# RWKV-5 and mixture of depths on one core: a bonus summed by the tensor engine, and rank counts with one compare a block

## The chip, the cores and the metric

The kernel runs on one core of one Trainium2 chip. The metric is the device time of one execution in microseconds (us). The core's engines are PE (TensorE, matrix products; PEld is its weight load), DVE (VectorE), ACT (ScalarE), POOL (GpSimd) and SP (SyncE, which issues most DMAs). Each runs its own queue of instructions in order and waits on semaphores for the others.

## The reference

Batch 4, 8 heads, 768 steps, 48 channels a head. First a linear attention with decay `w` and a bonus `u` for the current step, then a router which picks the 128 best tokens of each batch and passes only these through a small MLP (F = 1024).

```python
for t in range(S):
    cur = einsum('bhd,bhe->bhde', u[None] * kt, vt)
    y[:, :, t] = einsum('bhd,bhde->bhe', rt, state + cur)
    state = w[None, :, :, None] * state + einsum('bhd,bhe->bhde', kt, vt)
# x = y as (B, S, 384)
scores = einsum('bsd,d->bs', x, w_gate)
out = x.copy()
for b in range(B):
    top_idx = argpartition(-scores[b], capacity)[:capacity]
    ye = maximum(x[b, top_idx] @ w1, 0.0) @ w2
    g = 1.0 / (1.0 + exp(-scores[b, top_idx]))
    out[b, top_idx] = x[b, top_idx] + g[:, None] * ye
```

The bonus of a step is one number a head, the sum over the 48 channels of r·u·k, which multiplies v of the same step.

## The kernel before, in words

The work is cut into 24 units of 128 steps (`NU`; `NC` = 6 units a batch, `T` = 128), each with all 8 heads as `NP` = 4 pairs. The tokens of a unit are cut once more into two chunks of 64. The order of all instructions is written out by hand (`manual_schedule`), so every engine's queue is the order in which the functions are called. One turn of the main loop, iteration n, works on three units at once:

- `states(n-1)` (L322): what earlier chunks give to unit n-1, into the PSUM tiles y0 and y1, of which there is one each. A tiny ACT copy, the mark (L326), follows.
- `products(n)` (L282): k·v sums of both chunks, into the PSUM tile rp. `scores(n)` (L292): r·k inside a chunk, into other columns of rp.
- `added(n, c)` (L303, DVE): the running state plus a chunk's sum. For c = 1 four ACT activations scale it into z of the next unit (L310); the last unit of a batch has no c = 1.
- `masked(n)` (L297, DVE): copies the scores below the diagonal from rp over `at`, whose diagonal holds the bonus.
- `values(n-1)` (L338): at times v, added into y0 and y1. `finish(n-1)`: three ACT copies (L355, L357) take y0 and y1 to x, and SP stores x.
- `turn(n+1)`: transposes keys (L260) and r (L265) to put channels on partitions; ACT copies the keys to kh (L270), and `turned` (L275, DVE) scales r to rh.
- For the bonus: `bonus(n+2)` (L237, L243) multiplies r, k and u on POOL with the tokens on partitions, `bonus_sum(n+1)` (L247) reduces over channels on DVE to du, and `diagonal(n+1)` (L251, POOL) spreads du on the diagonal of `at`. `scaled(n+2)` (L233, POOL) scales the keys to kw.

The routing of a batch goes with the units of the next. `score(n-1)` (L367, DVE) is the router's score. For each block j of 128 tokens `scores_along` (L378, PE) turns the scores into a row, and `compare` (L385, L387, DVE) compares this row with each of the j+1 blocks so far, one instruction each, and counts. `count` and `rank` (L392, L396, L399, L402) give each token its rank; `match` (L423) makes a one-hot of the rank, `pick` (L429) its token and score, `fetch` (L445, POOL's indirect DMA) the token's row xr. `hidden` (L472) and `expert` (L481) are the MLP on PE, in pieces from iteration 11 on; `leave` (L489, L491) stores the result. The call `work_at(n, where)` inserts these pieces.

SP's loads of unit n+4 (`load`, parts 0 to 3: k, r and two halves of v) are each held until a named DVE instruction is done, and so are the 16 pieces of w1 and w2 (`weights`), two in each of iterations 6 to 13. r and k have five buffers, v has six.

Of the kernel before, what the change touches and what calls it, by code (L numbers as in the profile page):

```python
# [7 lines left out]
F32 = mybir.dt.float32  # L8
# [9 lines left out]
def kernel(  # L18
# [52 lines left out]
    nc.vector.memset(mark, 0.0)  # L71
    ub = const.tile([128, H, D], F32)
    wg = const.tile([128, Dm], F32)
    for i, q in enumerate((nc.sync, nc.scalar)):
        q.dma_start(
            out=wp[i * PAD : i * PAD + D, 0, :],
            in_=bass.AP(tensor=w.tensor, offset=w.offset + i * D, ap=[[1, D], [2 * D, NP]]),
        )
    nc.scalar.activation(mark, mark, AF.Sigmoid)
# [48 lines left out]
    load(0, 1)  # L128
    nc.sync.dma_start(out=ub, in_=bass.AP(tensor=u.tensor, offset=u.offset, ap=[[0, 128], [D, H], [1, D]]))
    load(0, 2)  # L130
# [58 lines left out]
    for i in range(NW - 1):  # L189
        nc.vector.tensor_mul(wp[:, i + 1, :], wp[:, i, :], wp[:, i, :])  # L190
        h = 1 << i
        if h < MID:
# [4 lines left out]
                         back[:, None, :, None].to_broadcast([128, 2, NP, MID]))  # L197
    wc = wp[:, NW - 1, :]
    gone = const.tile([128, 1], F32)
    nc.gpsimd.tensor_copy(gone, tr[:, 0, 0:1])  # L200
# [7 lines left out]

    counts = [const.tile([128, NC, NC + 2], F32, name=f"counts{i}") for i in range(2)]
    slots = const.tile([128, 128], F32)  # L210
# [3 lines left out]
    def late_tables():  # L214
        nc.gpsimd.iota(slots, pattern=[[1, 128]], base=0, channel_multiplier=0,
                       allow_small_or_imprecise_dtypes=True)
        for x in counts:
            nc.gpsimd.memset(x, 0.0)
            nc.gpsimd.iota(x[:, :, NC + 1], pattern=[[128, NC]], base=0, channel_multiplier=0,
                           allow_small_or_imprecise_dtypes=True)  # L220
        nc.gpsimd.iota(tok[:, :, 0], pattern=[[0, NU]], base=0, channel_multiplier=1,
                       allow_small_or_imprecise_dtypes=True)
        nc.gpsimd.iota(tok[:, :, 1], pattern=[[T, NU]], base=0, channel_multiplier=0,
                       allow_small_or_imprecise_dtypes=True)
# [4 lines left out]

    KH, RH, RK, RKU, DU, AT, ZA, ZB, YP = ({} for _ in range(9))  # L230

    def scaled(n):
        nc.gpsimd.tensor_mul(kws[n % 3][:, :, :D], KIN[n], wk)  # L233

    def bonus(n):
        rk = RK[n] = work.tile([128, H, D], F32, name="rk")
        nc.gpsimd.tensor_mul(rk, rpads[n % NIN][:, :, :D], KIN[n])  # L237
        if n:
            bonus_scaled(n, nc.gpsimd)

    def bonus_scaled(n, engine):
        RKU[n] = work.tile([128, H, D], F32, name="rku")
        engine.tensor_mul(RKU[n], RK[n], ub)  # L243

    def bonus_sum(n):
        DU[n] = work.tile([128, 2, NP], F32, name="du")
        return nc.vector.tensor_reduce(DU[n], RKU[n].rearrange("t (p i) d -> t i p d", i=2), axis=AX.X, op=OP.add)  # L247

    def diagonal(n):
        AT[n] = work.tile([128, H, C], F32, name="at", bufs=3)  # L250
        nc.gpsimd.tensor_mul(AT[n], dia[:, None, :].to_broadcast([128, H, C]),  # L251
                             DU[n].rearrange("t i p -> t (i p)")[:, :, None].to_broadcast([128, H, C]))

# [121 lines left out]
    def scores_along(b, j):  # L375
        p = psum.tile([128, 512], F32, name="m", bufs=4)
        SR[b, j] = p[:, :128]
        nc.tensor.transpose(SR[b, j], sc[b][:, j : j + 1].to_broadcast([128, 128]), ident)  # L378

    def compare(b, j):  # L380

        if j == 0:
            GT[b] = work.tile([128, NC, NC, 128], BF16, name="gt")
        for c in range(j + 1):
            nc.vector.tensor_scalar(GT[b][:, c, j, :], SR[b, j], sc[b][:, c : c + 1], None, op0=OP.is_gt, op1=OP.add,  # L385
                                    accum_out=counts[b % 2][:, c, j : j + 1])
        nc.vector.scalar_tensor_tensor(scr[:, :128], SR[b, j], sc[b][:, j : j + 1], earlier, op0=OP.is_equal,  # L387
                                       op1=OP.mult, accum_out=counts[b % 2][:, j, NC : NC + 1])

# [3 lines left out]

    def rank(b):
        p = psum.tile([128, 512], F32, name="m", bufs=4)
        nc.tensor.matmul(out=p[:, 0:1], lhsT=GT[b][:, 0, 0, :], rhs=ones[:, 1:2], start=True, stop=True)  # L396
        for c in range(1, NC):
            for cc in range(c):
                nc.tensor.matmul(out=p[:, c : c + 1], lhsT=GT[b][:, cc, c, :], rhs=ones[:, 0:1],  # L399
                                 start=(cc == 0), stop=(cc == c - 1))  # L400
        q = work.tile([128, NC], F32, name="qq")
        nc.vector.tensor_add(q, p[:, :NC], QQ[b])  # L402
        QQ[b] = q
# [11 lines left out]

    def match(b, z):
        oh = OH[b, z] = work.tile([128, NC, 128], BF16, name="oh")
        q = QQ[b]
        if z:
            q = work.tile([128, NC], F32, name="qz")  # L420
            nc.vector.tensor_scalar(q, QQ[b], float(-128 * z), None, op0=OP.add)
        for c in range(NC):
            nc.vector.tensor_scalar(oh[:, c, :], slots, q[:, c : c + 1], None, op0=OP.is_equal, op1=OP.add,  # L423
                                    accum_out=found[:, c : c + 1])
# [117 lines left out]

    bonus(0)
    warm(10)
# [5 lines left out]
    turned(0, pr)  # L550
    bonus_scaled(0, nc.vector)
    bonus_sum(0)
    earlier = const.tile([128, 128], F32)
    nc.vector.tensor_scalar(earlier, jp, 0.0, None, op0=OP.is_lt)
    ones = const.tile([128, 2], BF16)
    nc.vector.memset(ones[:, 0:1], -1.0)
    nc.vector.memset(ones[:, 1:2], 0.0)
    scaled(0)
    diagonal(0)
    scaled(1)  # L560
    bonus(1)
    for n in range(NU):
        if n == 2:
            late_tables()
        b, c = divmod(n, NC)
        if c == 0:
            ZA[n] = zt
        if n:
            behind = states(n - 1)
        products(n)  # L570
        scores(n)
        work_at(n, "scores")
        load(n + 4, 0, added(n, 0))
        op = masked(n)
        load(n + 4, 2, op)
        weights(2 * (n - NC), op)
        if n:
            values(n - 1, behind)
            finish(n - 1)
        if n + 1 < NU:  # L580
            pr = turn(n + 1)
        if c < NC - 1:
            added(n, 1)
        if n + 1 < NU:
            load(n + 4, 1, turned(n + 1, pr))
            load(n + 4, 3, bonus_sum(n + 1))
        if n + 2 < NU:
            scaled(n + 2)
        if n + 1 < NU:
            diagonal(n + 1)  # L590
        if n + 2 < NU:
            bonus(n + 2)
        work_at(n, "turn")
        if n:
            weights(2 * (n - NC) + 1, score(n - 1))
        if n + 1 < NU:
            work_at(n, "end")
# [71 lines left out]
```

## Time and profile before

| | us |
|---|---|
| median of 3 runs | 172.78 |
| lowest, highest | 168.68, 177.97 |
| the profiled execution | 166.79 |
| its span, first to last instruction | 165.0 |
| PE busy | 148.1 |
| DVE busy | 123.6 |
| POOL busy | 116.5 |
| ACT busy | 72.3 |

The mean granted clock of PE was 0.969 in this execution. A line of the page's groups gives the line of code, the engine and operation, the tile written and those read, the shape, the count, then busy time in us and the mean in ns of one, then the engine's idle time ahead of these and what ended it. A line of a timeline gives the start in us, the duration, the engine, the line and the operation; a line of the chain of waits gives the start, the time on the chain, and what ran.

### The profile page before, as it was taken

The numbers are of one execution on the slowest core, as the hardware profiler recorded it, in microseconds if no ns is written. First come the engines' busy times: TensorE is split into PE (matmuls) and PEld (weight loads), VectorE is DVE, ScalarE is ACT, GpSimd is POOL, SyncE is SP. The second block draws the span as 40 slices with busy tenths as digits, with TensorE's granted clock in tenths as the row PEclk, the third lists the DMA queues.
The fourth block names the chain that finished last, engine by engine and source line by source line (L and its number), as shares of the span: only waits on it lengthen the run. The fifth ranks groups of instructions, "written<-read, shape, count | busy, mean of one in ns | idle before, by whom it ended". The sixth has DMA issues, their size and how long they took to land.

```text
span 165.0 us, 7987 instructions
## 1 busy us (share of the span) xinstructions
PE 148.1 (90%) x3278; PEld 122.0 (74%) x3278; DVE 123.6 (75%) x478; ACT 72.3 (44%) x227; POOL 116.5 (71%) x158
## 2 busy tenths in 40 slices
PE   6869998887798599999999989999999978999970
PEld 2468887775686598999868859999787758968830
DVE  7854887989999948979999599799986987801010
ACT  6813765536455334454545244347524632202100
POOL 8499999998988897959878699968897621122002
PEclk9987999999999759999999999999999999999999
DMA  4988987978898899879988789978701321011001
GB/s 78 205 173 166 180 176 171 198 138 177 185 224 209 183 241 246 173 181 225 215 181 195 185 199 264 197 155 174 193 4 54 92 89 67 0 48 50 2 0 48
DMA packets 84325, 24.51 MB, mean 149 GB/s; under 512 B 76481, under 2 KB 83905, under 8 KB 84289
## 3 DMA queue, kind: packets, MB, share of 16 engines
q1 hardware_dynamic: 83568, 22.42, 61.0%
q0 software_dynamic: 512, 1.57, 3.1%
q8 instruction: 26, 0.43, 1.1%
q14 instruction: 11, 0.08, 0.1%
q10 hardware_dynamic: 208, 0.00, 0.1%
HBM read 18.48 MB, written 5.51 MB: 145 GB/s over the span
## 4 chain that ended last, share of the span: by engine, by line
PE 45%; POOL 16%; DVE 13%; issue 12%; DMA 5%; ACT 5%; POOLq 1%; ACTq 0%; DVEq 0%
PE m L472 9%; PE rp L282 7%; PE y L322 5%; PE m L260 5%; PE rp L292 5%; PE y L338 5%; PE m L265 4%; POOL rk L237 4%; PE m L481 4%; POOL at L251 4%; DVE gt L385 4%; POOL rku L243 3%; DMA rpad<-in_r_dram 3%; POOL kw L233 3%; ACT vpad L156 2%
## 5 line engine op out<-in xcount | busy, mean ns | idle before, releaser
L251 POOL TENSOR_TENSOR at<-dia,du 128x512 f32<-128x512 f32 x24 | 25.6, 1066 | 12.5 <-DVE du L247 10.3
L243 POOL TENSOR_TENSOR rku<-rk,ub 128x384 f32<-128x384 f32 x23 | 25.4, 1104 | 1.8
L385 DVE TENSOR_SCALAR_CACHE_REDUCE gt<-m,sc 128x128 bf16<-128x128 f32 x84 | 24.5, 344 | 1.3 <-PE m L378 1.3
L237 POOL TENSOR_TENSOR rk<-rpad,kin 128x384 f32<-128x384 f32 x23 | 24.3, 1056 | 1.3 <-DMA rpad<-in_r_dram 1.3
L367 DVE SCALAR_TENSOR_TENSOR scr<-x,wg 128x384 f32<-128x384 f32 x24 | 21.9, 912 | 2.6 <-DVE scr L387 0.5
L282 PE MATMUL rp<-vpad,kw 128*48 128x96 f32 x384 | 22.0, 260 | 1.9 <-POOL kw L233 1.2
L310 ACT ACTIVATE z<-g,wp 128x48 f32<-128x48 f32 x80 | 20.2, 326 | 7.3 <-DVE g L303 7.3
L472 PE MATMUL m<-xt,w 128*128 128x128 f32 x192 | 23.3, 276 | 0.0
L233 POOL TENSOR_TENSOR kw<-kin,wk 128x384 f32<-128x384 f32 x23 | 23.0, 1001 | 0.1
L472 PEld LDWEIGHTS m<-xt,w 128*128 128x128 f32 x192 | 22.3, 192 | 0.5 <-ACT xt L463 0.5
L481 PE MATMUL m<-w,ht 128*128 128x384 f32 x64 | 22.6, 491 | 0.1
L355 ACT COPY x<-y 128x192 f32<-128x192 f32 x24 | 7.7, 319 | 29.9 <-PE y L338 29.6
L282 PEld LDWEIGHTS rp<-vpad,kw 128*48 128x48 f32 x384 | 17.1, 129 | 3.8 <-POOL kw L233 1.7
L275 DVE TENSOR_TENSOR rh<-m,tables 112x512 f32<-112x512 f32 x24 | 16.4, 685 | 4.2 <-PE m L265 3.3
L322 PE MATMUL y<-g,rh 48*64 48x48 f32 x384 | 17.6, 230 | 0.7 <-ACT x L357 0.3
L297 DVE COPY_PREDICATED at<-mask,rp 128x512 f32<-128x512 uint32 x24 | 17.6, 735 | 0.7 <-POOL at L251 0.7
L292 PE MATMUL rp<-rh,kh 48*64 48x64 f32 x768 | 17.1, 228 | 0.0
L322 PEld LDWEIGHTS y<-z,rh 48*64 48x64 f32 x320 | 12.6, 139 | 5.4 <-issue 3.5
L292 PEld LDWEIGHTS rp<-rh,kh 48*64 48x64 f32 x768 | 13.8, 138 | 3.3 <-issue 0.3
L322 PE MATMUL y<-z,rh 48*64 48x48 f32 x320 | 15.6, 228 | 0.6 <-issue 0.4
L338 PE MATMUL y<-vpad,at 64*64 64x48 f32 x768 | 15.8, 221 | 0.4 <-ACT mark L326 0.4
L260 PE MATMUL m<-ident,kw 128*112 128x128 f32 x92 | 15.6, 294 | 0.6 <-POOL kw L233 0.6
(94 smaller groups left out, 251.0 us busy)
## 6 DMA issues: line engine op xcount, KB each, us to landing
rpad<-in_r_dram SPq DMA_DIRECT2D x24, 192.0 KB, 4.2
vpad<-in_v_dram SPq DMA_DIRECT2D x48, 96.0 KB, 4.2
out_dram<-x SPq DMA_DIRECT2D x24, 192.0 KB, 3.7
kin<-in_k_dram SPq DMA_DIRECT2D x23, 192.0 KB, 4.4
w<-in_moe_w_dram SPq DMA_DIRECT2D x16, 192.0 KB, 4.1
k<-in_k_dram SPq DMA_DIRECT2D x1, 192.0 KB, 2.8
ub<-in_u_dram SPq DMA_DIRECT2D x1, 192.0 KB, 4.0
wg<-in_moe_w_gate_dram SPq DMA_DIRECT2D x1, 192.0 KB, 4.3
```

The source lines that it names most:

```text
L233: nc.gpsimd.tensor_mul(kws[n % 3][:, :, :D], KIN[n], wk)
L237: nc.gpsimd.tensor_mul(rk, rpads[n % NIN][:, :, :D], KIN[n])
L243: engine.tensor_mul(RKU[n], RK[n], ub)
L251: nc.gpsimd.tensor_mul(AT[n], dia[:, None, :].to_broadcast([128, H, C]), DU[n].rearrange("t i p -> t (i p)")[:, :, None].to_broadcast([128 ...
L260: nc.tensor.transpose(pk[:CH, hp, :], two_heads(kws[n % 3] if keys is None else keys, hp), ident)
L282: nc.tensor.matmul(out=rp[i * PAD : i * PAD + D, hp // 2, at : at + 2 * D], lhsT=kws[n % 3][:, 2 * hp + i, :D], rhs=VIN[n][:, 2 * hp + i, ...
L292: nc.tensor.matmul(out=rp[ts, i, hp * C : (hp + 1) * C], lhsT=KH[n][rows, hp, ts], rhs=RH[n][rows, hp, ts], start=True, stop=True)
L322: mm = nc.tensor.matmul(out=YP[n][i][j * C : (j + 1) * C, hp * D : (hp + 1) * D], lhsT=RH[n][rows, hp, c * C : (c + 1) * C], rhs=z[rows, h ...
L338: mm = nc.tensor.matmul(out=YP[n][i][j * C : (j + 1) * C, hp * D : (hp + 1) * D], lhsT=AT[n][ts, i * NP + hp, :], rhs=VIN[n][ts, 2 * hp + ...
L385: nc.vector.tensor_scalar(GT[b][:, c, j, :], SR[b, j], sc[b][:, c : c + 1], None, op0=OP.is_gt, op1=OP.add, accum_out=counts[b % 2][:, c, ...
L472: nc.tensor.matmul(out=ph[:, f % 4, :], lhsT=w1[:, d, f * 128 : (f + 1) * 128], rhs=XT[b, z][:, d, :], start=(d == 0), stop=(d == KD - 1))
L481: nc.tensor.matmul(out=pe[:, :Dm], lhsT=HT[b, z][:, f, :], rhs=w2[:, f, :], start=(f == 0), stop=(f == FB - 1))
```

## The change

1. In units 0 to 10 (`TURNED` = 11) the bonus is no longer made with tokens on partitions. `turned_bonus` multiplies rh by kh, both already turned, in one product of 112x512, on POOL (unit 0 on DVE). `turned_sum` lets PE sum over the channels: the product is the stationary operand, a two-column table `uw` of u·w the moving one, four matmuls a unit into free columns of rp; ACT copies the result to du. From unit 11 on it stays as it was; `ub` is loaded in iteration 6 and no longer at the start, and the small table `uw` is loaded by two DMAs from ACT's queue.
2. In these units the second `added` moves up behind the first, `scaled(n+2)` and `diagonal(n)` follow it, and `masked(n)` comes behind `turned(n+1)`.
3. `compare` of block j is one instruction over all scores of the row so far, kept in `along`, a copy that ACT makes in `scores_along`. Counts are of lower scores instead of higher, so signs change in `rank`, `count` and `match`. The one-hot stays on DVE.
4. `score(n-1)` stands ahead of the pieces of routing of the same iteration. The load of the first v half comes behind that of r, and the second v half is held by `score`.

```diff
+    uw = const.tile([128, NP, 2], F32)
+    for i in range(2):
+        nc.scalar.dma_start(
+            out=uw[i * PAD : i * PAD + D, :, i],
+            in_=bass.AP(tensor=u.tensor, offset=u.offset + i * D, ap=[[1, D], [2 * D, NP]]),
+        )
...
-    nc.sync.dma_start(out=ub, in_=bass.AP(tensor=u.tensor, offset=u.offset, ap=[[0, 128], [D, H], [1, D]]))
...
+    nc.vector.tensor_mul(uw, uw, wp[:, 0, :, None].to_broadcast([128, NP, 2]))
...
+    def turned_bonus(n, engine):
+        RK[n] = work.tile([128, NP, T], F32, name="rkh")
+        engine.tensor_mul(RK[n][:CH], RH[n][:CH], KH[n][:CH])
+
+    def turned_sum(n):
+        at = NP * (C + D)
+        DU[n] = rp[:, 0, at : at + H].rearrange("t (i p) -> t i p", i=2)
+        for hp in range(NP):
+            nc.tensor.matmul(out=DU[n][:, :, hp], lhsT=RK[n][:CH, hp, :], rhs=uw[:CH, hp, :], start=True, stop=True)
+        if n:
+            du = work.tile([128, 2, NP], F32, name="du")
+            nc.scalar.copy(du, DU[n])
+            DU[n] = du
...
         nc.tensor.transpose(SR[b, j], sc[b][:, j : j + 1].to_broadcast([128, 128]), ident)
+        nc.scalar.copy(along[b % 2][:, j * 128 : (j + 1) * 128], SR[b, j])
...
-        for c in range(j + 1):
-            nc.vector.tensor_scalar(GT[b][:, c, j, :], SR[b, j], sc[b][:, c : c + 1], None, op0=OP.is_gt, op1=OP.add,
-                                    accum_out=counts[b % 2][:, c, j : j + 1])
-        nc.vector.scalar_tensor_tensor(scr[:, :128], SR[b, j], sc[b][:, j : j + 1], earlier, op0=OP.is_equal,
-                                       op1=OP.mult, accum_out=counts[b % 2][:, j, NC : NC + 1])
+        nc.vector.scalar_tensor_tensor(scr[:, :128], SR[b, j], s, onward, op0=OP.is_equal, op1=OP.mult,
+                                       accum_out=cnt[:, j, 1:2])
+        nc.vector.tensor_scalar(GT[b][:, j, : (j + 1) * 128], along[b % 2][:, : (j + 1) * 128], s, None, op0=OP.is_lt,
+                                op1=OP.add, accum_out=cnt[:, j, 0:1])
...
         products(n)
         scores(n)
+        if n < TURNED:
+            turned_sum(n)
         work_at(n, "scores")
         load(n + 4, 0, added(n, 0))
-        op = masked(n)
-        load(n + 4, 2, op)
-        weights(2 * (n - NC), op)
+        if n < TURNED:
+            if c < NC - 1:
+                added(n, 1)
+            if n > 2:
+                scaled(n + 2)
+            diagonal(n, nc.gpsimd if n else nc.vector)
+            if n <= 2:
+                scaled(n + 2)
+        else:
+            op = masked(n)
         if n:
             values(n - 1, behind)
             finish(n - 1)
         if n + 1 < NU:
             pr = turn(n + 1)
-        if c < NC - 1:
+        if c < NC - 1 and n >= TURNED:
             added(n, 1)
         if n + 1 < NU:
             load(n + 4, 1, turned(n + 1, pr))
-            load(n + 4, 3, bonus_sum(n + 1))
-        if n + 2 < NU:
+            if n + 1 < TURNED:
+                turned_bonus(n + 1, nc.gpsimd)
+        if n < TURNED:
+            op = masked(n)
+        load(n + 4, 2, op)
+        weights(2 * (n - NC), op)
+        if TURNED <= n + 1 < NU:
+            op = bonus_sum(n + 1)
+        if TURNED <= n and n + 2 < NU:
             scaled(n + 2)
-        if n + 1 < NU:
+        if TURNED <= n + 1 < NU:
             diagonal(n + 1)
-        if n + 2 < NU:
+        if TURNED <= n + 2 < NU:
             bonus(n + 2)
...
+        if n:
+            op = score(n - 1)
+            weights(2 * (n - NC) + 1, op)
+        load(n + 4, 3, op)
         work_at(n, "turn")
-        if n:
-            weights(2 * (n - NC) + 1, score(n - 1))
```

## The prediction

> **What bounds the kernel now.** I read the page first (engines, slices), then the costliest groups, then the chain of waits window by window, then the timelines of single engines.
>
> ```profile
> PE 148.1 (90%) x3278; PEld 122.0 (74%) x3278; DVE 123.6 (75%) x478; ACT 72.3 (44%) x227; POOL 116.5 (71%) x158
> ...
> L251 POOL TENSOR_TENSOR at<-dia,du 128x512 f32<-128x512 f32 x24 | 25.6, 1066 | 12.5 <-DVE du L247 10.3
> L243 POOL TENSOR_TENSOR rku<-rk,ub 128x384 f32<-128x384 f32 x23 | 25.4, 1104 | 1.8
> L385 DVE TENSOR_SCALAR_CACHE_REDUCE gt<-m,sc 128x128 bf16<-128x128 f32 x84 | 24.5, 344 | 1.3 <-PE m L378 1.3
> L237 POOL TENSOR_TENSOR rk<-rpad,kin 128x384 f32<-128x384 f32 x23 | 24.3, 1056 | 1.3 <-DMA rpad<-in_r_dram 1.3
> L472 PE MATMUL m<-xt,w 128*128 128x128 f32 x192 | 23.3, 276 | 0.0
> L233 POOL TENSOR_TENSOR kw<-kin,wk 128x384 f32<-128x384 f32 x23 | 23.0, 1001 | 0.1
> ...
> L355 ACT COPY x<-y 128x192 f32<-128x192 f32 x24 | 7.7, 319 | 29.9 <-PE y L338 29.6
> ```
>
> No engine bounds the whole run, so read it by stage. PE's 90% is an average: from the start of unit 2's DVE work (19.5 us) to about 60 us, PE has no expert matmuls and waits; from 65 us to 134 us the chain is nearly all PE. The timeline's sum g<-rp (L303, one pair a unit) gives each unit's beat: 15.84 us for unit 1, 19.46 for unit 2, 59.71 for unit 10, so 4.9 us a unit. In units 2 to 5 the chain runs through POOL's four operations (1.07+1.10+1.06+1.00 = 4.2 us), in units 6 to 9 through DVE. In units 17 to 22 the beat is PE's own: L322, L282, L292, L338, L260, L265 plus pieces of L472 or L481:
>
> ```profile
> 108.88 0.61 PE y L322 x32
> 109.49 0.80 PE rp L282 x16
> 110.28 0.62 PE rp L292 x32
> 110.91 0.45 PE y L338 x32
> 111.36 0.58 PE m L260 x4
> 111.94 0.44 PE m L265 x4
> ```
>
> That is 3.5 us of recurrence a unit. So the change can win only before 65 us, and there the order of ACT matters, which has 44% busy time and looks free:
>
> ```profile
> 19.82 0.32 ACT L355 COPY x<-y 128x192 f32<-128x192 f32 x1 [1.05 <-PE y L338]
> 20.16 0.64 ACT L357 COPY x<-y 64x192 f32<-64x192 f32 x2
> 20.82 0.58 ACT L270 COPY kh<-m 112x512 f32<-112x512 f32 x1
> 21.30 1.01 ACT L310 ACTIVATE z<-g,wp 128x48 f32<-128x48 f32 x4
> 22.21 0.17 ACT L326 COPY mark<-tables 1x1 f32<-1x1 f32 x1
> ```
>
> The reader is to see that x (the copy that empties y0 and y1) starts as soon as values (L338) is done, and takes 1.00 us to kh's start; z comes after, 0.91 us. The next states (L322) write y0 and y1 again, and start at 20.83, when x has just ended (20.80).
>
> [...] L472 (128 fp32 columns, 128 moving) comes every 0.112 us, and 15 bf16 matmuls with one moving column (L399) took 0.38 us, 25 ns each. [...]
>
> **The change part by part.** Times are full-clock durations of the rows.
>
> *POOL, units 0 to 10.* rk and rku go (1.06+1.10), one product rkh of 112x512 comes. Its nearest row is L251, 128x512, 1.07 us (1.00 to 1.3 as bounds). POOL: 4.2 to 3.1 us a unit.
> *DVE.* The reduction du goes: 0.46 us a unit. A block with j+1 compares took 0.27 us each by the timeline's spacing (344 ns with overlap, accumulator read included); one compare of (j+1)x128 columns is 0.13 us a block (L193 takes 426 ns for 256 columns, L196 691 for 512, 1.03 ns each) plus the remaining 0.14, so 0.93 instead of 1.62 at six blocks, 0.35 on average. Nothing of this lies on the path after 65 us.
> *ACT.* A copy of du (about 0.20, like L437's 203 ns) in units 1 to 10, and a copy `along` of 128x128 for each block, 0.27 (L355 has 0.32 at 192 columns).
> *PE.* turned_sum: 4 fp32 matmuls, two instructions each as for L472 (192 for 96), each with a new stationary of 128 columns and 2 moving. [...] 0.17 until a reader can start (L399's last to qq). Bounds: 8 x 25 ns = 0.2 and 8 x 0.112 = 0.9.
>
> *The order.* This decides. In units 0 to 10 the second sum added(n,1) moves up to just behind the first, so on ACT z(n+1) now stands ahead of x(n-1); and in the built program added(n,0) waits for the copy du(n), which waits for turned_sum(n). Behind z in ACT's queue stand x(n-1) and kh(n+1). states(n) wait for x(n-1), since y0 and y1 are single. Follow it from t = 0, the end of turned_sum(n):
>
> - du on ACT 0.05 to 0.25; the two sums g on DVE, 0.30 to 0.91 (0.27 to the next start, then 0.34)
> - z on ACT 0.94 to 1.85; x(n-1) 1.85 to 2.86 (values ended at 0.5 already and would have let it start then)
> - states(n) 2.88, products(n+1) 3.5, scores(n+1) to 4.91 (0.61+0.80+0.62)
> - turned_sum(n+1) and its latency 0.92: 5.83
>
> Beside it, and hidden: turn(n+1) on PE until 1.5; rh 1.55 to 2.2, masked(n) 2.2 to 2.9 (its diagonal on POOL 0.3 to 1.4); score(n-1) must wait for x: 2.9 to 3.45; kh to 3.35, along to 3.6; the compare 3.65 to 4.85 at most; rkh on POOL 3.45 to 4.5, ready before 4.91; the next scaled to 5.5, before the next diagonal at 6.1. So the loop is a ring of 5.8 us through PE, ACT, DVE, ACT, PE, above the present 4.9; POOL and DVE have slack they cannot use. Only unit 5 has no second sum, so no z: its x starts at 0.6, states at 1.65, scores end at 3.8, beat 4.7.
>
> *Start.* Two more DMA issues on ACT at 0.41 us each (the wp issue's row) stand ahead of the table load and of the copies that end in wk at 7.82; kw(0) then starts at 8.7 instead of 7.90. at(0) leaves POOL, and kw(1) comes no later than now. turned_sum(0), and kh(1) behind z(1), come onto the path: the end of turned_sum(1) falls at 16.9, where scores(1) now end at 15.7: +1.2.
>
> *Units 1 to 11.* Eight beats of 5.83 and one of 4.7 are 51.3 us: turned_sum(10) ends at 68.2, and scores(11), 4.9 later (no turned_sum), at 73.1. Now they end at 64.5. So +8.6. DVE's one-hot in unit 8 (six at 0.27, on DVE as before) would end at 5.9 of 6.1: just covered; if it isn't, +0.3 once.
>
> *Units 11 on.* The PE chain is the same. What the change can give back: before unit 17 PE waited 0.6 for xr, which POOL had started late since rk waited 1.33 us for rpad at 91.6. SP's order now puts rpad ahead of the v half and the weights, and score, which released the weights, stands ahead of the compares. I count -1.0 with some DVE stalls. DMA share falls in the slower stage, so loads are no new bound; each iteration still issues the same seven, half of them later (v behind masked and score), with four units of lead.
> *Tail.* The last two blocks: before, x(23) ended at 137.7, score at 139.3, gt to 141.7, qq at 142.17. Now along stands behind x on ACT, 137.7 to 138.0, compare to 139.0, score to 139.6, along to 140.4, compares to 141.6, count, qq at 142.2. What the compares save, the copies and their waits cost: 0.
>
> Sum: 8.6 - 1.0 = +7.6 on the profiled execution's 166.79 (span 165.0 and 1.8 around it): 174.4, which is 4.5% more. The median of the three runs, 172.78, lies 6.0 above that execution (168.68 to 177.97; PE's clock was granted at 0.969 in the profile, with dips in the slices from 8 to 16 and from 54 to 62 us). I carry the difference over: 172.78 + 7.6 = **180.4 us**.
>
> **The rivals.**
>
> *Cheap loads (0.20).* The same ring, but the eight weight loads come at the bf16 pace: beat 4.91 + 0.2 + 0.17 = 5.28, short one 4.2, 46.4 for nine, turned_sum(1) at 16.3: scores(11) at 67.6, +3.1, less 1.0: +2.1, 174.9. For it: L338's instructions follow each other in 14 ns with 64-column loads. [...]
> *It does what it says (0.08), the other side.* ACT's queue holds nothing up, that is, x is not behind z in effect or states do not wait for it, and POOL and DVE set the beat now. Then the next bound is PE's own 3.6 us, the beat of unit 1 to 2, plus 0.75: 4.4. Nine beats are 39.6 instead of 43.8, and with -1.0 later: -5, 168. It decides when the end of x lies less than 1.8 us behind turned_sum. Against: each link of the ring is in the built order.
> *Late pieces stack on the ring (0.12).* The compare, waiting for along, and score, waiting for x, push g(n+1) on DVE out, or v loads released 1 us later come late from 35 us on: 0.5 a beat more, +12, 185.
>
> **How the numbers follow.** Ring as worked out 0.60, cheap loads 0.20, stacked 0.12, as intended 0.08. The likeliest gives 180.4. Its unknown, the loads (0.2 to 0.9), runs from +2 to +9; the three runs of before spread by 9 us, so I take 172 to 188, which leaves out most of the intended case and the far end of the last. A measurement of this kernel tells about 2% (3.4 us) from no change. Slower: 0.60 + 0.12 and a little of the cheap loads, 0.74; same: most of the cheap loads, 0.18; faster 0.08.
>
> **What would show it.** Right: ACT's timeline in units 2 to 10 shows du, four z, then x, with x's idle time no longer ended by L338 but none at all, and L322 waiting on ACT's x for over a microsecond; POOL's busy share in 20 to 60 us falls from 0.9 to about 0.55; L303's starts are 5.8 apart; eight turned_sum instructions take 0.75 us. From 73 us on everything is shifted alike. Wrong: starts of L303 under 5.0 apart, or turned_sum at 0.2 us.

## The result, and the profile after

| us | before | after |
|---|---|---|
| median | 171.91 | 192.06 |
| lowest, highest (4 runs each) | 168.68, 177.97 | 189.87, 195.83 |
| the profiled execution | 166.79 | 189.87 |
| its span | 165.0 | 188.0 |
| mean granted clock of PE in it | 0.969 | 0.921 |

The ratio is 1.126, with a 95% interval of 1.100 to 1.153; it compares only those executions of each kernel that lie within 1.5% of its fastest, and is therefore not the quotient of the two medians. The forecast was slower, at 180.4 us, 7.6 above the median then known; the kernel lost 20 us. The page of the changed kernel: engines, two rows of the slices, then groups.

```profile
PE 167.5 (89%) x3366; PEld 140.1 (74%) x3366; DVE 109.8 (58%) x350; ACT 78.0 (41%) x261; POOL 105.5 (56%) x144
...
PEclk9975555799999999999999999999999998899997
DMA  5997644455766988888898975985740132101101
...
L270 POOL TENSOR_TENSOR at<-dia,du 128x512 f32<-128x512 f32 x23 | 26.1, 1136 | 23.6 <-DVE du L251 12.2
...
L256 POOL TENSOR_TENSOR rkh<-rh,kh 112x512 f32<-112x512 f32 x10 | 12.7, 1271 | 22.1 <-ACT kh L290 13.8
...
L497 PE MATMUL m<-xt,w 128*128 128x128 f32 x192 | 24.3, 284 | 0.0
```

VectorE and POOL are relieved as meant (DVE 123.6 to 109.8 us, POOL 116.5 to 105.5), and PE has 19 us more "busy" time in 23 us more span. `rkh` (L256) takes 1.27 us. The row PEclk holds the surprise: from the third slice to the eighth the clock is down, for four of them at half. The row of before has a short dip there:

```profile
PEclk9987999999999759999999999999999999999999
```

ACT's timeline in unit 4, with the columns start, duration, engine, line, operation and, in brackets, idle time and its releaser:

```profile
43.20 0.17 ACT L265 COPY du<-rp 128x8 f32<-128x8 f32 x1 [1.84 <-PE rp L262]
44.19 1.01 ACT L330 ACTIVATE z<-g,wp 128x48 f32<-128x48 f32 x4 [0.82 <-DVE g L323]
45.10 0.30 ACT L375 COPY x<-y 128x192 f32<-128x192 f32 x1
45.42 0.64 ACT L377 COPY x<-y 64x192 f32<-64x192 f32 x2
46.08 0.59 ACT L290 COPY kh<-m 112x512 f32<-112x512 f32 x1
46.56 0.27 ACT L399 COPY along<-m 128x128 f32<-128x128 f32 x1
46.90 0.19 ACT L346 COPY mark<-tables 1x1 f32<-1x1 f32 x1
49.23 0.17 ACT L265 COPY du<-rp 128x8 f32<-128x8 f32 x1 [2.14 <-PE rp L262]
```

This is the predicted queue: du, four z, then x with no idle time ahead of it, then kh. Before, x was ahead of z and started when L338 (now L358) ended. The waits, "who <- whom: total us, times, longest":

```profile
ACT du L265 <- PE rp L262: 26.7, 10, 4.5
DVE g L323 <- ACT du L265: 17.7, 9, 4.7
...
ACT z L330 <- DVE g L323: 13.5, 10, 5.3
...
PEld y L342 <- ACT x L375: 5.6, 6, 1.4
```

The links of the ring stand there one by one: du waits for turned_sum, g for du, z for g, and states' first weights (L342) for x. PE's timeline at full clock, ahead of du at 49.23:

```profile
46.72 0.86 PE L302 MATMUL rp<-vpad,kw 128*48 128x96 f32 x15
47.51 0.69 PE L312 MATMUL rp<-rh,kh 48*64 48x64 f32 x32
48.14 1.05 PE L262 MATMUL rp<-uw,rkh 112*128 112x2 f32 x8
```

turned_sum takes 1.05 us to its modelled end and 1.09 us from its start to du's start. The starts of L323 in units 4 to 8 are 43.40, 49.43, 54.95, 60.98 and 67.00 us: a beat of 6.02, and 5.52 behind unit 5.

Now the stages, for PE: window, length, busy time, granted clock, DMA share, GB/s.

```profile
11.30:35.30 24.00, 23.17 (x341) 0.50 0.56 112
35.30:73.00 37.70, 32.49 (x834) 1.00 0.73 159
73.00:93.70 20.70, 16.72 (x427) 1.00 0.84 195
93.70:154.30 60.60, 60.40 (x1476) 1.00 0.63 146
154.30:188.00 33.70, 27.15 (x255) 0.91 0.10 36
```

From 11.3 to 35.3 us the clock is 0.50, although PE shows 23.17 of 24.00 us busy by its records, whose ends are modelled. The sums (L323) of units 1, 2 and 3 come there 7.8, 8.7 and 7.5 us behind those of the unit before, where the open clock gives 6.0. The same window of before:

```profile
11.30:35.30 24.00, 22.27 (x644) 0.93 0.86 178
```

The time at half clock, summed over windows of 0.2 us, is 10.3 us before, in stretches of 3.4 and 6.8 us, and 29.7 us after, of which 23.9 in one stretch. In all traces of this study a stretch that did not run into the end of the span was 3.41 us long or a multiple of it; such a step of 3.41 us is called a window below.

### The profile page after: what moved, and what is told of

It reads as the page before. It is cut to its first block, busy times and chain, and to the rows that moved or that the text cites. A ratio compares the mean times of both kernels' runs of the same rounds, so it can differ in the third digit from the quotient of the medians.

```text
span 188.0 us, 8017 instructions
## 1 busy us (share of the span) xinstructions
PE 167.5 (89%) x3366; PEld 140.1 (74%) x3366; DVE 109.8 (58%) x350; ACT 78.0 (41%) x261; POOL 105.5 (56%) x144
## 4 chain that ended last, share of the span: by engine, by line
PE 66%; ACT 10%; issue 10%; DVE 8%; POOL 3%; POOLq 1%; ACTq 1%
PE rp L302 11%; PE m L497 9%; PE rp L312 8%; PE rp L262 7%; PE m L506 6%; PE y L342 6%; PE m L280 6%; PE y L358 6%; PE m L285 5%; ACT z L330 3%; DVE g L323 2%; DVE at L317 2%; ACT vpad L162 2%; ACT x L377 2%; PE m L398 1%
## 5 line engine op out<-in xcount | busy, mean ns | idle before, releaser
L302 PE MATMUL rp<-vpad,kw 128*48 128x96 f32 x384 | 22.8, 265 | 5.4 <-DVE at L317 3.2
L330 ACT ACTIVATE z<-g,wp 128x48 f32<-128x48 f32 x80 | 20.2, 325 | 13.5 <-DVE g L323 13.5
L256 POOL TENSOR_TENSOR rkh<-rh,kh 112x512 f32<-112x512 f32 x10 | 12.7, 1271 | 22.1 <-ACT kh L290 13.8
L497 PE MATMUL m<-xt,w 128*128 128x128 f32 x192 | 24.3, 284 | 0.0
L497 PEld LDWEIGHTS m<-xt,w 128*128 128x128 f32 x192 | 23.5, 201 | 0.5 <-ACT xt L488 0.5
L323 DVE TENSOR_TENSOR g<-rp,z 128x192 f32<-128x192 f32 x20 | 7.1, 357 | 24.2 <-ACT du L265 17.3
L387 DVE SCALAR_TENSOR_TENSOR scr<-x,wg 128x384 f32<-128x384 f32 x24 | 18.9, 786 | 2.5 <-ACT x L377 2.5
L342 PE MATMUL y<-z,rh 48*64 48x48 f32 x320 | 16.4, 232 | 4.4 <-ACT x L375 3.8
L342 PEld LDWEIGHTS y<-z,rh 48*64 48x64 f32 x320 | 13.1, 142 | 9.3 <-ACT x L375 4.8
L342 PE MATMUL y<-g,rh 48*64 48x48 f32 x384 | 17.3, 233 | 2.5 <-ACT x L377 2.5
L317 DVE COPY_PREDICATED at<-mask,rp 128x512 f32<-128x512 uint32 x24 | 17.5, 729 | 2.0 <-POOL at L270 2.0
L358 PE MATMUL y<-vpad,at 64*64 64x48 f32 x768 | 17.4, 230 | 1.0 <-issue 0.7
L342 PEld LDWEIGHTS y<-g,rh 48*64 48x64 f32 x384 | 14.2, 144 | 3.3 <-ACT x L377 3.3
L409 DVE TENSOR_SCALAR_CACHE_REDUCE gt<-along,sc 128x128 bf16<-128x128 f32 (+5 forms) x24 | 16.2, 675 | 0.0
```

The costliest lines, as they stand in the source:

```text
L302: nc.tensor.matmul(out=rp[i * PAD : i * PAD + D, hp // 2, at : at + 2 * D], lhsT=kws[n % 3][:, 2 * hp + i, :D], rhs=VIN[n][:, 2 * hp + i, ...
L317: return nc.vector.copy_predicated(at, causal, rp[:, :, : NP * C].rearrange("s i (p t) -> s i p t", p=NP))
L330: nc.scalar.activation(ZA[n + 1][:, hp, :], g[:, hp, :], AF.Copy, scale=wc[:, hp : hp + 1])
L342: mm = nc.tensor.matmul(out=YP[n][i][j * C : (j + 1) * C, hp * D : (hp + 1) * D], lhsT=RH[n][rows, hp, c * C : (c + 1) * C], rhs=z[rows, h ...
L358: mm = nc.tensor.matmul(out=YP[n][i][j * C : (j + 1) * C, hp * D : (hp + 1) * D], lhsT=AT[n][ts, i * NP + hp, :], rhs=VIN[n][ts, 2 * hp + ...
L387: return nc.vector.scalar_tensor_tensor(scr, xa[b][:, c, :], 1.0, wg, op0=OP.mult, op1=OP.mult, accum_out=sc[b][:, c : c + 1])
```

## The experiments

Medians below stand beside that of the kernel before on the same chip (168.6 to 171.5 us).

### The ring

**Order alone.** The kernel before, with only the second sum moved up.

```diff
         load(n + 4, 0, added(n, 0))
+        if c < NC - 1 and n < 2 * NC - 1:
+            added(n, 1)
         op = masked(n)
...
-        if c < NC - 1:
+        if c < NC - 1 and n >= 2 * NC - 1:
             added(n, 1)
```

> The kernel before with only the order of the sums changed: added(n,1) and its four z behind added(n,0) in units 0 to 10, masked behind both; bonus, routing and compares as before. The prediction's ring without turned_sum and its copy is 5.83 - 0.92 = 4.9 us, as long as the beat of the kernel before: 171 to 173, no change that can be told. A rival: z ahead of x costs by itself, beat 5.4 or more in units 1 to 10: 176 to 178.

Measured: 174.18 us (170.95 to 176.12; before 169.48). ACT's timeline in unit 2:

```profile
20.84 1.01 ACT L310 ACTIVATE z<-g,wp 128x48 f32<-128x48 f32 x4 [1.97 <-DVE g L303]
21.76 0.29 ACT L355 COPY x<-y 128x192 f32<-128x192 f32 x1
22.08 0.64 ACT L357 COPY x<-y 64x192 f32<-64x192 f32 x2
22.74 0.59 ACT L270 COPY kh<-m 112x512 f32<-112x512 f32 x1
```

z stands ahead of x, and g (the first sum of a unit) comes every 4.88 us in units 1 to 3 (15.18, 20.06, 24.93) and 5.0 to 5.1 in units 4 to 8. The ring without turned_sum was put at 4.91. It is there, at about the beat that the kernel had. From unit 9 on this profile also loses to 10.2 us at half clock, so its total prices the order only loosely.

**The sum's length.** turned_sum in bf16.

```diff
-        RK[n] = work.tile([128, NP, T], F32, name="rkh")
+        RK[n] = work.tile([128, NP, T], BF16, name="rkh")
...
-    nc.vector.tensor_mul(uw, uw, wp[:, 0, :, None].to_broadcast([128, NP, 2]))
+    uwb = const.tile([128, NP, 2], BF16)
+    nc.vector.tensor_mul(uwb, uw, wp[:, 0, :, None].to_broadcast([128, NP, 2]))
...
-rhs=uw[:CH, hp, :]
+rhs=uwb[:CH, hp, :]
```

> The changed kernel with the product rkh and the table uw of turned_sum rounded to bf16 (so the bonus is less exact); all else the same. Theory 1, turned_sum's length is a term of the ring: 1.00 us becomes 0.3 to 0.4, the beat of 6.02 us becomes 5.3 to 5.4, eight beats give 5 us back, and more where the clock was at half: 184 to 187 instead of 192. Theory 2, the beat is set by ACT, DVE and POOL beside it and PE only waits less or more: beat above 5.9, 190 to 192.

Measured: 176.50 us (175.31 to 177.18; ratio 1.041, 1.034 to 1.048). Four matmuls take the place of eight, the beat is 5.23, and the half clock at the start lasts two windows. Of 15.6 us gained, the beat explains nine times 0.8, some 7; the rest I put down to the clock. Theory 1 holds for the beat; the gain is larger than its number.

**z behind x again**, in the changed kernel, and the start filled by ten more filler matmuls (products of a tile of zeros, whose result nobody reads), each alone and both.

```diff
# e1, z behind x
-            if c < NC - 1:
-                added(n, 1)
...
-        if c < NC - 1 and n >= TURNED:
+        if c < NC - 1:
             added(n, 1)
# e2, start filled
-    warm(4)
+    warm(14)
# e3: both edits
```

> The changed kernel with the second sum added(n,1), and with it the four z activations, put back behind turn in all units; nothing else. Ring theory: x is no longer behind z on ACT, so the beat of units 3 to 8 (starts of the first g on DVE) falls from 6.0 to about 4.7 us, set by masked, scores and turned_sum; nine beats save about 11 us: 177 to 179 us. Load theory (the weight loads of turned_sum are what made the beat long): the beat stays above 5.5, and the time within 4 us of 190. Clock theory (PE's half clock from 11 to 35 us is the larger loss): that stretch stays as it is, in both cases.

> The changed kernel with 14 instead of 4 dummy matmuls behind the first turn, so that PE isn't idle between 7.9 and 10.1 us; nothing else. Clock theory: PE's granted clock stays at 1.0 between 11 and 35 us, units 0 to 3 take 6 us each instead of 7.5 to 8.7, and 6 to 7 us are saved: 183 us. If turned_sum itself, with its loads and two moving columns, keeps the clock down: the clock falls to 0.5 all the same a few us later and the time stays within 2 us of 190.

> Both edits in one kernel: second sum and z behind turn, and 14 dummy matmuls. If the two causes are separate their savings add up: 190 - 11 - 6 = 172 to 174 us, near the kernel before. If the clock's loss came from the waits of the ring, e1 alone already has full clock and this one is no faster than e1.

Measured: e1 188.81 and 182.09, e2 185.16 (ratio 1.099, 1.080 to 1.118), e3 185.77 (1.103, 1.085 to 1.120). e2 kept the clock open until 77 us and had the beat of 6.03 from unit 1 on, with no filler in the ring itself: clock theory, 2 us short. e1 and e3 came out far from the ring's numbers, for two reasons. First, with z out of the way the beat at full clock is 5.5, not 4.7. DVE and PE in e3 show what took its place:

```profile
30.37 0.69 DVE L295 TENSOR_TENSOR rh<-m,tables 112x512 f32<-112x512 f32 x1 [0.68 <-PE m L285]
30.97 0.72 DVE L317 COPY_PREDICATED at<-mask,rp 128x512 f32<-128x512 uint32 x1
...
31.75 0.87 PE L302 MATMUL rp<-vpad,kw 128*48 128x96 f32 x16 [0.70 <-DVE at L317]
```

`masked` now stands behind rh, and products(n+1) wait 0.70 us for it. So PE's own path is a ring as well: turned_sum, values, both transposes, rh, masked, products, scores. Second, in e3 the clock opened and closed in turn from 39.7 to 63.6 us, one window at half, one at full; in e1, of which the slower execution was profiled, it did so from 24.7 to 52.0 us, and units 2 to 6 came every 6.72 to 6.80 us, nearly two windows each.

**All three edits.**

> The changed kernel with three edits at once: added(n,1) and z back behind the transposes, 14 filler matmuls instead of 4 at the start, product and table of turned_sum in bf16 (the bonus is less exact). Theory 1, the loss is the ring (fp32 sum and z ahead of x) and the half clock, and turned_sum in fp32 is also what let the clock flip every second window in the kernel with the first two edits: no flips before 60 us, beat 5.5 - 0.8 = 4.7, 170 to 172. Theory 2, the masked copy behind rh holds the products whatever turned_sum takes: beat 5.3 to 5.5 and 176 to 178.

Measured: 172.51 us (171.46 to 174.09; ratio 1.012, 1.003 to 1.022), beats of 4.69 to 4.87 in units 2 to 6, and about 4 us at half clock. With the sum short, neither ring is longer than the old beat, and the loss is nearly gone. Theory 2 falls.

### The half clock

**Fillers in two units only**, in iterations 1 and 2, that is, behind the transposes of units 2 and 3, while the clock was expected at half.

```diff
             pr = turn(n + 1)
+            if n in (1, 2):
+                warm(3)
```

> The changed kernel with three more filler matmuls (bf16, 128x512) behind the transposes of units 1 and 2, while the clock is at half. Theory 1, the clock opens by how much the array streams, and turned_sum with its two moving columns and the waits count little: the clock is back by about 25 us instead of 35, two units get 1.5 us shorter, the fillers cost some 1.3 us each: 189 to 191, with g(5) at 46 to 48 us instead of 49.4. Theory 2, PE is busy enough as it is (89 to 100% by the trace) and the stretch has another cause: the clock returns at 35 as before and the fillers are added, 193 to 195.

Measured: 186.97 us (182.82 to 190.19). Inconclusive: in the profiled execution the clock didn't close at the start at all (unit 1 at 18.05, before any filler), and then closed from 60.8 to 74.5 us, where there were none. The edit leaves the start alone, so where the clock closes differs from one execution to the next.

**Fillers in every turned unit**: the same three matmuls for all n < TURNED, in the time in which PE waits for x.

> The changed kernel with three filler matmuls (bf16, 128x512, some 0.25 us each at full clock) behind the transposes of each of units 1 to 11, in the time in which PE waits for x; the start is not touched. Theory 1, [...] fp32 matmuls with two moving columns stream little: half-clock stretches up to 75 us are one or two windows, never the 13 to 24 us seen so far, the mean clock is 0.95 or more in every execution, beat 6.0, 183 to 185. Theory 2, waits and small matmuls have nothing to do with it: stretches of 13 us and more again in some execution, clocks of 0.87 to 0.92, 189 to 193.

Measured: 181.71 us, and all four runs within 181.40 to 181.86 (ratio 1.068, 1.062 to 1.074). Added PE work makes the kernel 10 us faster, with the ring at 6.02 as before. But fillers close waits and stream columns at once. Three more kernels have other fillers in the same place:

```diff
+    def thin(k):
+        p = psum.tile([128, 512], F32, name="m", bufs=4)
+        for _ in range(k):
+            nc.tensor.matmul(out=p[:, :2], lhsT=ident, rhs=ident[:, :2], start=True, stop=True)
...
             pr = turn(n + 1)
+            if n < TURNED:
+                thin(3)
# e17: out=p[:, :128], lhsT=ident, rhs=ident
# e16: lhsT=busy[:, :128], rhs=busy[:, :2], thin(7)
```

> The changed kernel with three fp32 matmuls of two moving columns (as turned_sum's, some 0.75 us together) behind the transposes of each of units 1 to 11, where the run before had three bf16 matmuls of 512 columns (0.65 us); both stand in the time in which PE waits for x. Theory 1, the clock goes by how much the array streams: these don't keep it open, stretches of 13 us and more at half clock appear, mean clocks under 0.93, 189 to 194, in some executions at least. Theory 2, the clock goes by whether PE has work at all: as good as the wide ones, 181.5 to 183 with clocks of 0.98.

> As the run with three fp32 matmuls of two moving columns in PE's waits (220 us, once 181.6), but with 128 moving columns in each: the same stationary, the same type, as many instructions, and by the rows seen so far nearly as long (0.112 to 0.125 us an instruction[...]). If the columns streamed decide: clock open, 181.5 to 183 in every execution. If fp32 decides: 215 to 221 again in most.

> The same fillers with seven bf16 matmuls of two moving columns on a bf16 stationary, some 0.7 us a unit. If the columns streamed decide: half-clock stretches as long as with the thin fp32 ones, 200 us or more in most executions. If the type decides (bf16 keeps the clock open, as the wide bf16 fillers did): 181.5 to 183.

| fillers in units 1 to 11 | median us | each run's mean clock | at half clock in the profile, us |
|---|---|---|---|
| none (the changed kernel) | 192.06 | 0.921, 0.897, 0.905, 0.872 | 29.7 |
| 3 bf16, 512 columns | 181.71 | 0.983 to 0.989 | 5.4 |
| 3 fp32, 128 columns | 180.25 | 0.982, then 0.997 to 0.998 | 6.3 |
| 3 fp32, 2 columns | 220.03 (once 181.56) | 0.745, 0.746, 0.745, 0.983 | 111.2 |
| 7 bf16, 2 columns | 188.20 | 0.926, 0.941, 0.936, 0.897 | 27.6 |

Window 14.8 to 35.3 us in the profiles with 3 fp32 fillers of 2 columns and of 128 columns, in this order: length, then busy time of PE, PEld, DVE, ACT and POOL with instructions, the clock, DMA share, GB/s; then each one's PEclk row.

```profile
14.80:35.30 20.50, 20.50 (x281) 19.10 (x283) 6.73 (x14) 6.55 (x25) 7.77 (x12) 0.50 0.46 97
...
14.80:35.30 20.50, 19.03 (x456) 16.96 (x457) 9.50 (x27) 8.95 (x34) 12.33 (x16) 1.00 0.70 146
```

```profile
PEclk9955555555555555555557999999999999889998
...
PEclk9999999999999999969999999999999999999996
```

The two kernels differ in one number, the moving columns; stationary, type and count are the same. (They ran on different chips; the kernel before took 171.49 and 168.62 us there.) With 2 columns PE is busy 20.50 of 20.50 us by the trace and stays at half clock for 105.8 us; the window that ends this stretch, from 113.8 to 117.2 us, is in unit 11, which has neither turned_sum nor fillers. With 128 columns it shows 19.03 of 20.50 and a clock of 1.00. So fp32 as such doesn't shut the clock (1.00 with 128 columns), and time that the trace counts as PE's waiting isn't what keeps it shut (none with 2 columns); what is left is the number of moving columns, 2 against 128. The thin bf16 fillers show no gain clear of the noise (ratio 1.104, 1.089 to 1.119, on the chip of the wide fp32 ones): their type alone doesn't help. They take 0.32 to 0.37 us a unit, not 0.7, so they don't show how long ones would do. The one execution of the thin fp32 fillers in which the clock stayed open (181.56, mean 0.983) is as fast as the wide ones: in that kernel the clock seems to stay as it is, open or shut.

The other profiles bear on this, one execution each. In eight of the 18 the clock closed at the start, at 11.0 to 12.4 us. It opened again after one window in the kernel before and in e4 (the routing alone, below), two with the sum in bf16 (e7), four in e1, six in e10 (below) and e16, seven in the changed kernel, and 31 with the thin fp32 fillers. In this order the number of two-column fp32 instructions in a unit rises: none in the first three, eight in the next four, fourteen in the last. Of the six kernels with more fillers at the start none closed there; of the twelve others four didn't.

What stays open is whether wide fillers open a shut clock. In both profiles that have them in every unit it didn't close at the start, before the first filler ran (at 13.5 and 13.3 us), and e2 kept it open until 77 us without any in the ring. What speaks for it is that all nine executions with them have a mean clock of 0.982 or more.

### The routing

**The routing part alone**, on the kernel before: one compare a block over along, score ahead of the routing. And its complement, the changed kernel with the routing of before.

```diff
# e4, on the kernel before: scores_along, compare, rank, match, late_tables as in the change, and
+        if n:
+            weights(2 * (n - NC) + 1, score(n - 1))
         work_at(n, "turn")
-        if n:
-            weights(2 * (n - NC) + 1, score(n - 1))
# e10, on the changed kernel: scores_along, compare, rank, match, late_tables as before
```

> The kernel before with the routing part of the change alone: one compare a block over the row copied by ACT, changed signs, score ahead of the routing pieces; bonus, order of sums and loads as before. All theories: not the cause of the slowdown. From DVE's 4.0 to 3.6 us a unit I expect units 6 to 9, which DVE sets, to gain 0.2 to 0.4 us each, and the rest to stay on PE: 1 to 2 us less than the kernel before, 170 us. If the copies and waits for along on ACT cost something, it would be 1 to 2 us slower.

> The changed kernel with the routing of the kernel before: one compare for each pair of blocks, no copy along; the order of the loop, score ahead of the routing, and the bonus as in the changed kernel. If the routing's gain of 1.4% seen alone on the kernel before adds to the bonus's loss, this is 2 to 3 us slower than the changed kernel: 194 to 195. If DVE is hidden wherever the ring sets the beat, the routing gives little here: 192, within 1.

Measured: e4 168.40 us over 18 runs, ratio 0.986 (0.981 to 0.992): a gain of 1.4% over before, small but clear of noise. Which of its two edits, the single compare or the earlier score, brings it wasn't tested. Its units 2 to 10 come 4.54 us apart on average (15.88 to 56.76 us for nine beats), those of before 4.87. e10: 188.43 (185.23 to 193.24), not slower than the changed kernel. The routing's gain exists where DVE sets the beat, and is swallowed where the ring does.

**Can it be bettered?** e9 adds five fillers at the start to e4, e12 also loads the weights two iterations earlier, e14 adds to e9 three wide fillers in units 8 to 11.

```diff
# e9, on e4
-    warm(4)
+    warm(9)
# e12, on e9
-        weights(2 * (n - NC), op)
+        weights(2 * (n - NC) + 4, op)
...
-            weights(2 * (n - NC) + 1, score(n - 1))
+            weights(2 * (n - NC) + 5, score(n - 1))
# e14, on e9
             pr = turn(n + 1)
+            if 7 <= n < 2 * NC - 1:
+                warm(3)
```

> The kernel before with the routing part of the change alone (one compare a block over along, score ahead of the routing) and 9 filler matmuls instead of the 4 at the start, to carry PE over its idle stretch at 8 us. If the one window at half clock from 11 to 15 us is on the path, 1 to 1.5 us less than the routing part alone (168.4): 167. If the fillers delay the transposes of unit 0 as much, 168 to 169.

> As the kernel with the routing part alone and 9 filler matmuls, with each piece of w1 and w2 loaded two iterations earlier (two in each of iterations 4 to 11). In the routing kernel PE stands still from 61.5 to 64.1 us for xr and unit 13's r, with the DMA engines 0.85 busy. If the bunching of the weights there is the cause, unit 11 to 12 takes 6 instead of 9.1 us: 164 to 165. If transfers are the bound over the whole first 100 us, the wait only moves: 167 to 168.

> The kernel before with the routing part of the change alone, 9 filler matmuls instead of 4 at the start, and three (bf16, 128x512) behind the transposes of units 8 to 11. If the half clock at 55 to 59 us is on the path, 1 to 2 us less than without the last fillers: 166 to 167. If transfers (xr, unit 13's r) set the time there, the stall at 62 us grows by as much: 168 to 169.

Measured: e9 168.45 (ratio 0.980, 0.968 to 0.993), e12 170.93 (1.002), e14 171.03 (1.007, 1.002 to 1.012). In e9 the window at half clock at the start is gone, but g of unit 2 comes at 19.36 us instead of 19.50: nothing on the path came sooner. e4's POOL shows what is late instead:

```profile
64.69 1.00 POOL L237 TENSOR_TENSOR rk<-rpad,kin 128x384 f32<-128x384 f32 x1 [2.60 <-DMA rpad<-in_r_dram]
```

It waits 2.60 us for unit 13's r. In e12 the stall only moved (unit 9 to 10 takes 8.3 us, and the clock is at half there, so transfers alone don't price it), and in e14 unit 11 to 12 takes 11.3. Both second theories had the direction, and both kernels came out slower still than their figures. In e4 the transfer is late ahead of the experts, by those 2.60 us. Of these kernels e4 and e9 beat both kernels of the case; the data don't rank them.

## Why the prediction was right or wrong

**Right: the mechanism.** The ring through PE, ACT, DVE, ACT and PE sets the beat: 6.02 us against 5.83 worked out; without turned_sum 4.88 to 5.1 against 4.91, which alone proves little, since the old beat was as long; with a cheap sum 5.23 against the rival's 5.28. The wait of states for x, forecast at over a microsecond, shows as 0.55 us (unit 4, at 45.45), since PE fills the time ahead of it with the transposes of the next unit. turned_sum's length was forecast nearly rightly: from its start to du's it took 1.09 us, where the ring has 0.92. The 0.75 us in that 0.92, for the eight instructions, was the author's estimate between the bounds of 0.2 and 0.9 us from the rows, and no trace showed it; the eight took 1.05 us to their modelled end, some 0.13 us each, and PEld's timeline has their weight loads running for 0.97 us of it (48.14 to 49.11). The rival's cheap loads, 0.2 us, are out. rkh took 1.27 us against 1.07 and was still just covered (46.74 to 48.01, turned_sum at 48.14).

**Wrong: the size.** The sum for the profiled execution was 174.4 and the execution took 189.87, 15.5 more. In the order of the prediction's terms:

- *"Times are full-clock durations of the rows"*: +7.0. The copy du, which waits for turned_sum(10), starts at 80.2 us, where the sum's end was forecast at 68.2: 12.0 late. With wide bf16 fillers it starts at 71.9, with the same ring. Of these 8.3 us, 1.3 are unit 8's (below) and 7.0 the clock's, in units 0 to 3. This is the failed step. The page of before showed the clock dip at the start, and the prediction saw dips only as a reason for the spread. It did not ask what the new matmuls do to the clock. The kernel before also falls to half at 11.4 us and is back after one window; the changed one stays there for seven, 23.9 us at 0.50. At half clock turned_sum takes 1.87 us, and the ring's other PE parts 1.6 to 1.8 times as long as at full clock. e2, which only fills the start, shows that these 7 us are the clock's: its ring is the changed kernel's, its clock is open until 77 us, and its sum g of unit 10 comes at 71.87 us, with the wide fillers at 72.08, in the changed kernel at 80.38.

```profile
27.82 1.87 PE L262 MATMUL rp<-uw,rkh 112*128 112x2 f32 x8
```

- *DVE's one-hot in unit 8, "just covered"*: +1.3 in this execution (7.30 us from unit 8 to 9). The transposes of unit 9 came 0.9 us late, for which the trace shows no cause, so rh did, and score behind it started when POOL already ran rkh. It took 1.46 us instead of 0.56 and ended 0.4 us after rkh did (72.04 and 71.62). With the wide fillers, score had ended before rkh began, took 0.56, and the beat was 6.03: covered.
- *Start and units 1 to 10 at full clock*: +3.7. Nine beats: eight times 0.2, and unit 5 at 5.52 instead of 4.7, since products(n+1) wait for masked, which the prediction had counted as hidden; together 2.4. Unit 1 is 1.1 late; with the wide fillers products(1) wait 0.56 us for masked there, and I didn't follow the rest.
- *scores(11), "4.9 later"*: +1.6. The change back to the old bonus puts rk and rku of unit 11, and xr's fetch, on POOL's queue ahead of kw and of `at` of unit 10:

```profile
78.87 1.00 POOL L245 TENSOR_TENSOR rk<-rpad,kin 128x384 f32<-128x384 f32 x1
79.95 1.00 POOL L247 TENSOR_TENSOR rku<-rk,ub 128x384 f32<-128x384 f32 x1
80.88 0.09 POOL L469 MEMSET spacer<- 1x1 f32 x1
81.15 1.17 POOL L470 DMA_INDIRECT xr<-out_dram,idx  x1 [0.18 <-DVE g L323]
82.36 1.01 POOL L241 TENSOR_TENSOR kw<-kin,wk 128x384 f32<-128x384 f32 x1
83.31 1.05 POOL L270 TENSOR_TENSOR at<-dia,du 128x512 f32<-128x512 f32 x1
...
84.39 0.73 DVE L317 COPY_PREDICATED at<-mask,rp 128x512 f32<-128x512 uint32 x1 [1.95 <-POOL at L270]
...
85.18 0.87 PE L302 MATMUL rp<-vpad,kw 128*48 128x96 f32 x16 [1.41 <-DVE at L317]
```

masked (L317) waits 1.95 us for that `at`, and products 1.41 us for masked. The prediction had POOL's steady order in this place, not its queue in iterations 9 and 10. The fetch itself is 1.17 us of it.
- *From scores(11) on, -1.0, and tail 0*: +1.9. From the end of scores(11) the execution took 103.2 us against 102.3 before. PE's clock was 0.91 in the last 33.7 us, where it was 1.00 before. Why it closed once more there wasn't tried.

The median adds the other way: the prediction carried over 6.0 us between profiled execution and median, and the changed kernel's is 2.2. 15.5 - 3.8 = 11.7, the miss. It is partly luck, therefore, that the kernels with the clock held open have medians of 180.3 and 181.7, next to the forecast of 180.4: the 6.0 made up for the smaller terms.

The sign "everything is shifted alike from 73 us on" held within 1.6 us: units 11 to 23 came 20.5 to 22.1 us later than before.

**The clock.** How busy PE is by the trace doesn't tell when the clock closes or opens: the longest gap in PE's records ahead of the first closing was 1.24 us (before) and 2.2 us (after), and with thin fp32 fillers PE was busy without a gap from 20.0 to 117.4 us and stayed at half clock until 117.2. The measurement decides. What closes and opens the clock isn't settled by these runs; that it goes by streamed columns was the author's theory, and the runs show it only for the fillers of 2 and of 128 columns (105.8 us at half clock from the start, and none there).

## What to carry to other kernels

Before a reduction is moved to the tensor engine, count what its matmuls stream as well as what they last: with two moving columns turned_sum took 1.05 us, with weight loads running for 0.97 of it, and the kernel that has it stood at half clock for 23.9 us, in which PE's other work in the ring took 1.6 to 1.8 times as long. If PE waits in a ring anyway, wide filler matmuls in that wait are worth trying (192.06 to 181.71 us here); a mean clock well below that of the kernel before is the sign (0.872 to 0.921 here, against 0.969). And when a sum moves ahead of another in one engine's queue, follow the ring that it closes: take each part away alone (order, length of the sum) and compare the beats, not the totals.

## What the runs showed of the hardware

- PE stayed at half clock for 105.8 us while its records left no gap, with three fp32 fillers of two columns a unit (e15); one execution of four of that kernel ran at a mean clock of 0.983 (181.56 us against 220). With 128 columns in the same places (e17), five executions took 180.0 to 181.5 us at mean clocks of 0.982 to 0.998.
- Once shut at the start, the clock came back after one window of 3.41 us in the kernel before, seven in the changed one and 31 with those thin fillers (e15).
- Two moving columns took about as long an instruction as 128, with fp32 stationaries of 128 columns: turned_sum's eight instructions took 1.05 us, six of L149 with 128 columns (e17) 0.83, some 0.13 and 0.14 us each.
- The half clock alternated with the full one, window by window, from 39.7 to 63.6 us in e3, and from 24.7 to 52.0 us in the profiled execution of e1 (mean clock 0.904), where the beats were 6.72 to 6.80 us over five units.
- Adding instructions to an engine that waits was worth 10 us: 192.06 to 181.71 us with three wide matmuls a unit (e13).
